# RWKV6 attention and a mixture of adapters: tiles of 64 tokens of two sequences, r and k held transposed

## The chip, the cores and the metric

The kernel runs on one core of a Trainium2 chip. The metric is the device time of one execution in microseconds (us), the median of the runs. The core has five engines with instruction streams of their own: PE (TensorE, the matrix array of 128 rows by 128 columns), DVE (VectorE), ACT (ScalarE), POOL (GpSimd) and SP (SyncE, which here only issues transfers). They meet through semaphores. PSUM is the accumulator memory that PE writes; SBUF is the working memory.

## The reference

Linear attention with a decay per channel (4 batches, 8 heads, 768 tokens, 48 channels per head), then a mixture of adapters over the 3072 tokens with all heads side by side (384 columns). All inputs and the output are fp32.

```python
for t in range(S):                                          # attention, state: (B, H, D, D)
    cur = np.einsum('bhd,bhe->bhde', u[None] * kt, vt)
    y[:, :, t] = np.einsum('bhd,bhde->bhe', rt, state + cur)
    state = wt[:, :, :, None] * state + np.einsum('bhd,bhe->bhde', kt, vt)
...
logits = x @ w_gate                                         # x = y as (3072, 384); 8 experts
topk = np.argpartition(-logits, K, axis=1)[:, :K]           # K = 2
sel = np.take_along_axis(logits, topk, axis=1)
w = np.exp(sel - sel.max(-1, keepdims=True))
w /= w.sum(-1, keepdims=True) + 1e-09
for e in range(E):
    z = x[mask] @ A[e]                                      # 384 -> 16
    delta[mask] += w[mask, k, None] * (z @ B[e])            # 16 -> 384
return x + delta
```

## The kernel before

The recurrence is done in chunks. With P the prefix sum of log w along the tokens of a chunk, r is multiplied by exp(P - centre) and k by exp(centre - P). The attention inside a chunk is then a masked product (r k^T) v, and what earlier chunks give is r times the state. The state S is accumulated as k^T v in PSUM over all chunks of a sequence; the prefix sums run on through the sequence by a second matmul on the chunk before, so nothing has to be rescaled. The term with u is computed apart, as a number per token and head, r.(u k), times v.

**Tiles.** A tile is 128 tokens of one sequence with all 8 heads: 24 tiles, 6 for each of the 4 sequences, one sequence after the other. Tokens lie on the partitions, (head, channel) along the free side. These are the steps of a tile, each a function of the same name:

- `load_w` (two tiles, L168), `load_rk` (r and k, 128x768 fp32, one DMA, L178) on SP; `load_v` (groups of `VGROUPS`, cast to fp16 on the way, L183) on POOL's queue.
- `ln` and `ln1` (ACT, two tiles at once, L245, L254), `cs` (the prefix sums for r and for k, four matmuls of 384 columns with triangular matrices, L257), `exps` (ACT, 128x768, fp32 out, L269), `mult` (DVE, r and k times the exponentials, fp32 in, bf16 out, L274). The output has 64 columns for each head of 48; the padding is set to zero once (memset, L230, four buffers).
- `tr` and `trev`: r and k are transposed, two heads at a time, by 8 PE transposes of 128x128 (L307), and copied out by ACT (128x1024, L316). Afterwards heads of even number lie on partitions 0 to 47, those of odd number on 64 to 111.
- `amm` (8 matmuls of 48 rows, 128x128 out, L321), `aev` (DVE, the mask, 128x1024, L331).
- `kv` (8 matmuls of 64 columns each onto the state, L337, L344), `sev` (ACT, the state to bf16, L347).
- `ymm`: 4 matmuls of r and the state (96 columns, L358) and 8 of the masked products and v (48 columns, L364), all into one PSUM tile y_ps.
- `rkp` (POOL, r times k, L282), 3 transposes of it, `dgmm` (3 matmuls with u, L287), `dgev` (ACT, two tiles, L294), `dv` (POOL, v times that number, L301).
- `xev` (DVE, dv + y_ps to xs, fp16, L368): the tile's attention output.
- `xk` (L374): 3 transposes of xs, and with them the 3 of the rkp of the tile `LEAD` = 3 ahead; `xkev` (L382): their copy, by ACT and DVE in turn.
- `lgmm` (the gate's logits, L393). For a batch of tiles (`BATCHES`, four as a rule): `gate` (ACT, L398), `gmax` (DVE, L405), `gsel` (POOL, four small operations, L417), `zmm` (x times all A, L426), `zw` (DVE, times the gate, L435), `zT` and `zTev` (its transposes, copied by DVE, L444, L452).
- `dmm` (identity times xs, plus zT times all B, into d_ps, L459), `oev` (ACT, to res, L465), `store` (SP, one DMA of 192 KB per tile, L470).

**Order.** The order in which each engine gets its instructions is written by hand. `plan` (L127) gives step f of tile t the due time t + `OFFSET[f]` + `EXTRA[f, t]`, sorts all of them and emits them in that order; the scheduler keeps it on PE, ACT, DVE, POOL and SP. An engine that waits holds up all that stands behind it on its own queue. PSUM tiles are named buffers: one each for cs_ps, s_ps (the state, the logits and the numbers of the u term), trp and a_ps, and a pair with the tag "y" that serves y_ps, xk_ps, z_ps, zT_ps and d_ps in turn.

Of the kernel before, what the change touches and what calls it, by code (L numbers as in the profile page):

```python
# [8 lines left out]
F32 = mybir.dt.float32  # L9
# [9 lines left out]
NCHUNK = 6  # L19
NTILE = 24  # L20
AHEAD = 12
BATCHES = (4, 4, 4, 4, 4, 3, 1)

LEAD = 3
VGROUPS = {0: 1, 1: 3, 4: 4, 8: 4, 12: 4, 16: 4, 20: 4}
VBUFS = {4: 5}
STAGES = ("load_w", "load_rk", "load_v", "ln", "ln1", "cs", "exps", "mult", "rkp", "dv", "tr", "trev", "amm",
          "aev", "kv", "sev", "ymm", "xev", "xk", "xkev", "lgmm", "dgmm", "dgev", "adapters", "casts", "gate", "gmax",
          "gsel", "zmm", "zw", "zT", "zTev", "dmm", "oev", "store")
BATCHED = ("gate", "gmax", "gsel", "zmm", "zw", "zT", "zTev")  # L30

OFFSET = dict(
    load_w=-14.300,
    load_rk=-12.200,
    load_v=7.854,
    ln=9.443,
    ln1=9.187,
    cs=10.060,
    exps=10.665,
    mult=11.280,  # L40
    rkp=9.834,
    dv=13.417,
    tr=11.584,
    trev=12.172,
    amm=12.458,
    aev=12.748,
    kv=12.759,
    sev=13.487,
    ymm=13.577,
    xev=13.957,  # L50
    xk=14.425,
    xkev=14.657,
    lgmm=14.807,
    dgmm=11.851,
    dgev=12.302,
    adapters=-10.500,
    casts=11.924,
    gate=14.935,
    gmax=15.088,
    gsel=15.729,  # L60
    zmm=15.649,
    zw=16.167,
    zT=16.307,
    zTev=16.550,
    dmm=19.950,
    oev=20.325,
    store=159.956,
)
EXTRA = {
    ("load_v", 1): 1.652, ("load_v", 4): 2.471, ("load_v", 20): 0.905,  # L70
    ("ln", 0): -7.731,
    ("cs", 3): 0.370, ("cs", 19): 0.400, ("cs", 21): 0.100,
    ("exps", 4): -0.041,
    ("rkp", 20): 1.472, ("rkp", 21): -0.694,
    ("tr", 3): 0.115,
    ("trev", 1): -0.304, ("trev", 22): -0.410,
    ("amm", 1): -0.099,
    ("aev", 4): -0.018, ("aev", 22): 0.545, ("aev", 23): 0.306,
    ("kv", 22): 0.906, ("kv", 23): -0.729,
    ("sev", 22): 0.179,  # L80
    ("ymm", 20): 0.145, ("ymm", 22): -0.144,
    ("xk", -1): -0.293, ("xk", 0): 0.103,
    ("xkev", -2): 0.186, ("xkev", 2): 0.189,
    ("lgmm", 0): 1.315, ("lgmm", 2): 0.440, ("lgmm", 20): 0.808, ("lgmm", 23): 0.194,
    ("dgmm", 0): 0.907, ("dgmm", 3): 0.277,
    ("dgev", 23): 0.038,
    ("gate", 23): 0.088,
    ("gmax", 19): 0.423,
    ("zmm", 19): 0.638, ("zmm", 22): 0.554,
    ("zw", 19): 0.159, ("zw", 22): 0.214, ("zw", 23): 0.051,  # L90
    ("zT", 19): 0.119, ("zT", 22): 0.576,
    ("zTev", 19): 0.208, ("zTev", 22): 0.664,
    ("dmm", 19): -0.366,
}
TAG = {("d", NTILE - 2): "y", ("d", NTILE - 1): "a_ps", ("z", NTILE - 1): "trp"}
XK_ENG = ("ACT", "DVE")


def batches():
    at, lag, t0 = {}, {}, 0  # L100
    for n in BATCHES:
        at[t0 + n - 1] = (t0, n)
        for t in range(t0, t0 + n):
            lag[t] = t0 + n - 1 - t
        t0 += n
    return at, lag


def runs(f, t, gate_at):
    if f in BATCHED:  # L110
        return t in gate_at
    if f in ("kv", "sev"):
        return t % NCHUNK != NCHUNK - 1 or f == "kv" and t == NTILE - 1
    if f in ("adapters", "casts", "ln1"):
        return t == 0
    if f in ("ln", "load_w"):
        return t % 2 == 0 and not (f == "load_w" and t == 0)
    if f == "load_rk":
        return t > 0
    if f == "load_v":  # L120
        return t > 0 and t in VGROUPS
# [17 lines left out]
def kernel(  # L139
# [28 lines left out]
    def load_w(t):  # L168
        w_in = io.tile([L, 2, HD], F32, name="w_in", bufs=(AHEAD + 4) // 2)
        for i in range(2):  # L170
            st[t + i]["w"] = w_in
# [354 lines left out]
```

## Time and profile before

| | |
|---|---|
| median of 3 runs | 106.34 us (105.53 to 106.39) |
| the profiled execution, its own time: span from first to last instruction | 103.7 us |
| matmuls on PE | 1350, each with a weight load |
| DMA issues | 24 loads of r and k and 24 stores of 192 KB among them |

The profile is one execution, recorded by the hardware; its span runs from the first to the last recorded instruction. The median of the runs stands 2.6 us above that span.

A row of the timeline gives an instruction's (or a group's) start and length in us, its engine, its line in the kernel, the operation, the tile written and the tiles read, their shape (partitions x elements) and type, and a count. For PE, "48*128" ahead of a shape is the part of the array in use, rows times columns. In a table of groups the shape is followed by the count, then by busy time and the mean of one in ns, then by the idle time ahead of them and what ended it. Matmuls overlap, so a group's length is less than its count times the mean of one.

### The profile page before, as it was taken

To read this page: it belongs to the slowest core of one execution; us is meant where nothing else is said; L and a number is where in the kernel's file an instruction comes from. 1 tells how busy PE (TensorE), PEld (TensorE's weight loads), DVE (VectorE), ACT (ScalarE), POOL (GpSimd) and SP (SyncE) were. 2 spreads that over 40 slices of the span, in tenths; PEclk is the share of its full clock that TensorE was granted. 3 is DMA by queue.
4 is the path that set the end of the run, shared out by engine and by line. 5 is a ranking of instruction groups with operands and counts; after the bars stand their busy time and mean duration, and the time that the engine had idled before them with its cause. 6 is when DMAs were issued, how large, how long until landed. Compare 5 with 4: busy or idle time off the path is not lost.

```text
span 103.7 us, 3388 instructions
## 1 busy us (share of the span) xinstructions
PE 85.7 (83%) x1350; PEld 61.8 (60%) x1350; DVE 84.5 (81%) x147; ACT 81.2 (78%) x140; POOL 66.0 (64%) x99
## 2 busy tenths in 40 slices
PE   3455985999198999999968999999999999768640
PEld 0114564777085877777846787777877786645310
DVE  5516599899749999999999999989999999965600
ACT  4525997899559889999996999999999998444360
POOL 5716486959349799787971978939879072613300
PEclk9999999999999999999999999999999999999996
DMA  2999999999999999999659220179201222203353
GB/s 88 203 363 403 380 315 368 404 345 304 340 304 335 410 395 386 341 310 353 216 52 185 82 76 28 54 91 212 77 8 73 81 81 76 79 6 127 145 188 146
DMA packets 13679, 21.86 MB, mean 211 GB/s; under 512 B 1120, under 2 KB 10592, under 8 KB 13664
## 3 DMA queue, kind: packets, MB, share of 16 engines
q1 hardware_dynamic: 10480, 19.30, 51.1%
q0 software_dynamic: 3184, 2.36, 16.1%
q8 instruction: 10, 0.16, 0.7%
q14 instruction: 5, 0.04, 0.1%
HBM read 19.29 MB, written 4.72 MB: 231 GB/s over the span
## 4 chain that ended last, share of the span: by engine, by line
PE 32%; DMA 32%; DVE 15%; ACT 8%; issue 6%; SPq 1%; POOL 1%; ACTq 1%; DVEq 0%; POOLq 0%
DMA v_4_370<-in_v_dram 10%; DMA rk_in<-in_rk_dram 9%; DMA out_dram<-res 8%; DMA w_sb<-in_weights_dram 5%; PE trp L312 5%; DVE rk_1_121 L276 4%; DVE xs L370 3%; PE cs_ps L267 3%; PE cs_ps L265 3%; PE xk_ps L379 3%; ACT res L467 2%; PE a_ps L327 2%; PE d_ps L461 2%; PE s_ps L344 2%; PE z_ps L431 2%
## 5 line engine op out<-in xcount | busy, mean ns | idle before, releaser
L333 DVE TENSOR_TENSOR at<-a_ps,at_mask 128x1024 f16<-128x1024 f32 x24 | 29.2, 1216 | 2.1 <-PE a_ps L327 2.0
L284 POOL TENSOR_TENSOR rkp<-rk_in 128x384 f16<-128x384 f32 x24 | 23.9, 997 | 6.2 <-DMA rk_in<-in_rk_dram 6.0
L318 ACT COPY rkT<-trp 128x1024 bf16<-128x1024 bf16 x24 | 24.5, 1021 | 2.4 <-PE trp L312 2.2
L370 DVE TENSOR_TENSOR xs<-dv,y_ps 128x384 f16<-128x384 f32 x24 | 13.0, 543 | 1.4 <-PE s_ps L395 1.3
L467 ACT COPY res<-d_ps 128x384 f32<-128x384 f32 x24 | 11.6, 488 | 3.2 <-PE d_ps L462 2.7
L349 ACT CAST S_sb<-s_ps 128x384 bf16<-128x384 f32 x20 | 9.8, 488 | 2.9 <-PE s_ps L344 2.1
L250 ACT ACTIVATE logw<-w_in 128x768 f16<-128x768 f32 x11 | 9.4, 856 | 3.1 <-DMA w_in<-in_w_dram 3.1
L386 ACT COPY xkT<-xk_ps 128x768 f16<-128x768 f16 (+1 forms) x13 | 9.9, 762 | 0.4 <-PE xk_ps L379 0.2
L327 PE MATMUL a_ps<-rkT 48*128 48x128 bf16 x192 | 9.7, 222 | 0.3 <-ACT rkT L318 0.3
L267 PE MATMUL cs_ps<-logw,strict 128*128 128x384 f16 x24 | 8.3, 348 | 1.4 <-POOL at_mask masks.py:66 1.4
L379 PE MATMUL xk_ps<-ident_86,rkp 128*128 128x128 f16 x72 | 8.3, 226 | 1.2 <-POOL rkp L284 1.2
L388 DVE COPY xkT<-xk_ps 128x768 f16<-128x768 f16 (+1 forms) x14 | 6.9, 492 | 2.7 <-PE xk_ps L379 2.5
L379 PE MATMUL xk_ps<-ident_86,xs 128*128 128x128 f16 x72 | 8.0, 219 | 0.8 <-DVE xs L370 0.5
L267 PE MATMUL cs_ps<-logw,n_incl 128*128 128x384 f16 x24 | 8.4, 351 | 0.0
L461 PE MATMUL d_ps<-xs,ident_86 128*128 128x384 f16 x24 | 7.7, 323 | 0.4 <-ACT res L467 0.3
L265 PE MATMUL cs_ps<-logw,co_strict 128*128 128x384 f16 x20 | 6.8, 341 | 1.5 <-ACT e_210 L271 0.9
L462 PE MATMUL d_ps<-Ball,zT 128*128 128x384 f16 x24 | 7.8, 323 | 0.0
L379 PEld LDWEIGHTS <-xs 128*128 128x128 f16 x72 | 5.2, 97 | 3.9 <-DVE xs L370 1.9
L327 PEld LDWEIGHTS <-rkT 48*128 48x128 bf16 x192 | 5.5, 95 | 3.1 <-ACT rkT L318 0.5
L364 PEld LDWEIGHTS <-at 128*128 128x128 f16 x192 | 7.0, 96 | 0.4
L358 PE MATMUL y_ps<-S_sb,rkT 128*128 128x96 bf16 x80 | 6.8, 208 | 0.4 <-ACT res L467 0.4
L265 PE MATMUL cs_ps<-logw,n_co_incl 128*128 128x384 f16 x20 | 6.9, 346 | 0.0
(165 smaller groups left out, 220.6 us busy)
## 6 DMA issues: line engine op xcount, KB each, us to landing
rk_in<-in_rk_dram SPq DMA_DIRECT2D x24, 384.0 KB, 9.6
out_dram<-res SPq DMA_DIRECT2D x24, 192.0 KB, 1.9
w_in<-in_w_dram SPq DMA_DIRECT2D x11, 384.0 KB, 9.1
w_in<-in_w_dram SPq DMA_DIRECT2D x2, 192.0 KB, 2.4
v_4_370<-in_v_dram POOLq DMA_DIRECT2D x1, 384.0 KB, 10.4
v_4_510<-in_v_dram POOLq DMA_DIRECT2D x1, 384.0 KB, 10.8
v_4_839<-in_v_dram POOLq DMA_DIRECT2D x1, 384.0 KB, 11.3
v_4_1190<-in_v_dram POOLq DMA_DIRECT2D x1, 384.0 KB, 5.4
```

Source lines behind the costliest of these rows:

```text
L265: nc.tensor.matmul(o, lhsT=wa, rhs=st[t - 1]["logw"], start=False, stop=False, skip_group_check=True)
L267: nc.tensor.matmul(o, lhsT=wb, rhs=lw, start=False, stop=True, skip_group_check=True)
L284: nc.gpsimd.tensor_mul(p_, st[t]["rk"][:, 0], st[t]["rk"][:, 1])
L318: nc.scalar.copy(out=rkT, in_=st[t]["trp"])
L327: nc.tensor.matmul(a_ps[:, g, p, :], lhsT=rkT[base:base + D, 1, p, :], rhs=rkT[base:base + D, 0, p, :], start=True, stop=True)
L333: nc.vector.tensor_mul(at, st[t]["a_ps"].rearrange("s g p f -> s (g p) f"), at_mask.to_broadcast([128, H, 128]))
L349: nc.scalar.copy(out=sb, in_=S_acc)
L370: nc.vector.tensor_add(xs, st[t]["dv"].rearrange("p a b -> p (a b)"), st[t]["y_ps"].rearrange("p a b -> p (a b)"))
L379: nc.tensor.transpose(xk_ps[:, 3 * q + j, :], src[:, j * 128:(j + 1) * 128], ident16)
L386: nc.scalar.copy(out=sb[:, lo:hi], in_=st[t]["xk_ps"][:, lo:hi])
L461: nc.tensor.matmul(d_ps, lhsT=ident16, rhs=st[t]["xs"], start=True, stop=False)
L467: nc.scalar.copy(out=res, in_=st[t]["d_ps"])
```

## The change

A tile is now 64 tokens of two sequences at once. There are again 24 tiles, 12 for each pair of sequences (`NCHUNK` = 12). Nothing of what is computed changes.

- **Layout and loads.** The host lays r and k out with channels on the partitions (48 for even heads at 0, 48 for odd heads at 64) and, along the free side, sequence, head pair, r or k, and token: 1024 elements. `load_rk` fetches them in 8 groups (`RKGROUPS`), two DMAs each, on POOL's queue, cast to fp16 into four standing buffers. Tile 0 comes as fp32 by SP. Rows 48 to 63, which no load writes, are set to zero by memsets (`pads`, and some of the start). v and w are laid out so that a tile has 64 tokens of the one sequence above 64 of the other.
- **Prefix sums.** `cs` makes them transposed: for each head pair and sequence one matmul on the tile before (or on a constant) and one on this tile, 64 rows, 128 columns. `exps` reads 112x1024 and writes bf16; `mult` multiplies 112x1024 of 16-bit data; `rkp` is made on DVE out of the same data (112x512). `tr` and `trev` are gone.
- **Attention.** `amm`, `dgmm`, `kv`, `inter` and `intra` (which were `ymm`) become 16 matmuls each, for 2 sequences by 8 heads, on 64x64 quarters of the array. `kv` needs k with tokens on the partitions: `ktr` transposes it (16 of 64x64), `ktev` (DVE) copies it out. The mask product is 128x512.
- **The u term.** `dv` is written as fp16 and `bonus` adds it to y_ps on PE, by four matmuls with the identity. `xev` is then a plain copy, by ACT and DVE in turn.
- **Rest.** `xk` has 3 transposes, its copy is always DVE's. `gsel` is on DVE. `xk_ps`, `k_ps`, `z_ps`, `zT_ps` and `d_ps` share a ring of two PSUM buffers. The prefix sums of a tile lie in two banks, y_ps in two. Each store is two DMAs, of 64 rows. `res` has 8 buffers.
- **Order.** A written list (`ORDER`) takes the place of the due times.

```diff
-NCHUNK = 6
+NCHUNK = 12
+C = 64
-VGROUPS = {0: 1, 1: 3, 4: 4, 8: 4, 12: 4, 16: 4, 20: 4}
+VGROUPS = {0: 2, 2: 2, 4: 4, 8: 4, 12: 4, 16: 4, 20: 4}
+RKGROUPS = {1: (0, 1), 2: (0, 2), 4: (1, 2), 6: (1, 2), 8: (2, 4), 12: (3, 4), 16: (1, 4), 20: (2, 4)}
+RKBUF = {0: 3, 1: 4, 2: 4, 3: 4}
-OFFSET = dict(
...
+ORDER = """
+adapters.0 load_w.1 load_w.3 pads.1 pads.2 pads.3 ln.0 load_v.0 load_rk.1 casts.0 cs.0 ln.1 exps.0 mult.0 load_rk.2
+load_w.5 load_v.2 rkp.0 load_rk.4 cs.1 ln.3 exps.1 load_v.4 load_rk.6 rkp.1 cs.2 amm.0 mult.1 rkp.2 dgmm.0 ktr.0
+dgmm.1 exps.2 dgev.1 cs.3 dv.0 aev.0 intra.0 ktr.1 load_w.7 dv.1 ktev.0 exps.3 bonus.0 xev.0 dgmm.2 kv.0 mult.2
...
+dgmm.8 ktev.8 intra.7 xkev.6 bonus.7 dgmm.9 amm.8 sev.7 dmm.0 xev.7 mult.9 xk.7 lgmm.6 load_v.12 cs.10 oev.0 ktr.9
+dgev.9 rkp.10 inter.8 kv.8 aev.8 dv.8 xkev.7 exps.10 store.0 rkp.11 load_w.13 dv.9 amm.9 intra.8 bonus.8 dgmm.10
...
+zT.22 store.11 gmax.23 gsel.23 zTev.22 oev.17 zmm.23 dmm.18 zw.23 dmm.19 oev.18 zT.23 oev.19 store.12 dmm.20 zTev.23
+store.13 dmm.21 store.14 oev.20 dmm.22 store.15 oev.21 oev.22 dmm.23 store.16 oev.23 store.17 store.18 store.19
+store.20 store.21 store.22 store.23
+"""
...
+    nc.vector.memset(logws[0][:, :, :, D:], 0.0)
+    nc.vector.memset(rkbuf[0][32:64, 0:1], 0.0)
...
+    nc.vector.memset(rkbuf[0][32:64, 1:3], 0.0)
...
     def load_rk(t):
-        rk_in = io.tile([L, 2, HD], F32, name="rk_in")
-        nc.sync.dma_start(out=rk_in, in_=rk[t])
+        b, n = RKGROUPS[t]
+        o = t - 1 if b == 0 else t % 4
+        for g in range(2):
+            nc.gpsimd.dma_start(out=rkbuf[b][g * 64:g * 64 + D, o:o + n], in_=rk[g, :, t:t + n])
...
+    def pads(t):
+        nc.vector.memset(rkbuf[t][32:64], 0.0)
...
     def cs(t):
...
+        for p in range(P):
+            for b in range(2):
+                s = slice(b * 64, b * 64 + 64)
+                o = cs_ps[:, b, p].rearrange("a r t -> a (r t)")
+                if c == 0:
+                    nc.tensor.matmul(o, lhsT=ones[s, :], rhs=centre[s].rearrange("a r t -> a (r t)"),
+                                     start=(p == 0), stop=False, skip_group_check=True)
+                else:
+                    nc.tensor.matmul(o, lhsT=pre[s, p], rhs=carry[s].rearrange("a r t -> a (r t)"),
+                                     start=False, stop=False, skip_group_check=True)
+        for p in range(P):
+            for b in range(2):
...
+                nc.tensor.matmul(o, lhsT=lw[s, p], rhs=cur[s].rearrange("a r t -> a (r t)"),
+                                 start=False, stop=True, skip_group_check=True)
...
+    def mult(t):
+        rk2 = wk.tile([128, 2, P, 2, C], BF16, name="rk2", bufs=4)
+        nc.vector.tensor_mul(rk2[0:112].rearrange("a b p r t -> a (b p r t)"), st[t]["rk"][0:112],
+                             st[t]["e2"][0:112].rearrange("a b p r t -> a (b p r t)"))
...
+    def ktr(t):
+        k_ps = pp.tile([128, 2, P, D], BF16, name="k_ps", tag="ring", bufs=2)
+        for b in range(2):
+            for p in range(P):
+                for g in range(2):
+                    nc.tensor.transpose(k_ps[rows(g, 64), b, p, :], rk2[rows(g), b, p, 1, :],
+                                        identb[rows(g), 0:D])
...
+    def inter(t):
+        for p in range(P):
+            for b in range(2):
+                for g in range(2):
+                    nc.tensor.matmul(y_g[g][rows(b, 64), p, :], lhsT=d["rk2"][rows(g), b, p, 0, :],
+                                     rhs=st[t - 1]["S"][rows(g), p, b, :], start=(p == 0), stop=False,
+                                     skip_group_check=True)
...
+    def bonus(t):
+        for b in range(2):
+            for g in range(2):
+                nc.tensor.matmul(y_ps[rows(b, 64), g, 0:P * D], lhsT=ident[rows(g, 64), rows(g, 64)],
+                                 rhs=d["dv"][rows(g, 64), b].rearrange("s p d -> s (p d)"), start=False, stop=True,
+                                 skip_group_check=True)
...
     def store(t):
-        nc.sync.dma_start(out=out[t * 128:(t + 1) * 128, :], in_=st[t]["res"])
+        q, c = divmod(t, NC)
+        for b in range(2):
+            nc.sync.dma_start(out=out_v[q, c, b], in_=st[t]["res"][rows(b, 64)])
```

In `amm`, `ktr`, `dgmm` and `kv` the quarters used alternate between the upper left and the lower right of the array; in `inter` and `intra` they go round all four. (`intra` has the loops of `inter`, with the masked products and v.)

More of the change, by code (lines that the diff above doesn't have):

```diff
@@ L32 @@
-OFFSET = dict(
[L33 to L94, printed above, removed]
@@ L331, in aev @@
[L331 to L345 removed]
+        dv_ = wk.tile([L, 2 * P, D], FP16, name="dv", bufs=3)
@@ L376, in xk @@
[L376 to L379 removed]
+        xk_ps = pp.tile([128, 3, 128], FP16, name="xk_ps", tag="ring", bufs=2)
+        for j in range(3):
+            nc.tensor.transpose(xk_ps[:, j, :], st[t]["xs"][:, j * 128:(j + 1) * 128], ident)
         st[t]["xk_ps"] = xk_ps
```

465 lines of the change are left out of this document (243 added, 222 removed).

## The prediction

> **What bounds the kernel now.** I read the page's busy times first, then the pace of one operation through the span, then the timelines of PE, DVE and ACT inside the even stretch. Columns of a timeline are start, length (us), engine, line, operation.
>
> ```profile
> span 103.7 us, 3388 instructions
> ...
> PE 85.7 (83%) x1350; PEld 61.8 (60%) x1350; DVE 84.5 (81%) x147; ACT 81.2 (78%) x140; POOL 66.0 (64%) x99
> ```
> ```profile
> 16.72 0.54 DVE L370 TENSOR_TENSOR xs<-dv,y_ps 128x384 f16<-128x384 f32 x1
> ```
> ```profile
> 30.40 1.21 DVE L333 TENSOR_TENSOR at<-a_ps,at_mask 128x1024 f16<-128x1024 f32 x1
> 31.53 0.54 DVE L370 TENSOR_TENSOR xs<-dv,y_ps 128x384 f16<-128x384 f32 x1
> 31.99 0.36 DVE L412 MAX8 top<-ge 128x8 f32<-128x8 f32 x4
> ...
> 32.68 0.93 DVE L276 TENSOR_TENSOR rk_3_125<-rk_in,e_645 128x768 bf16<-128x768 f32 x1
> ...
> 35.12 0.68 DVE L438 TENSOR_TENSOR zw<-z_ps,g 128x512 f16<-128x512 f32 x1
> ...
> 36.59 0.41 DVE L455 COPY zT<-zT_ps 128x512 f16<-128x512 f16 x1
> 36.93 0.54 DVE L388 COPY xkT<-xk_ps 128x768 f16<-128x768 f16 x1
> ```
> ```profile
> 93.83 0.55 DVE L370 TENSOR_TENSOR xs<-dv,y_ps 128x384 f16<-128x384 f32 x1 [1.33 <-PE s_ps L395]
> ```
> The first xs (tile 0) starts at 16.72, that of tile 4 at 31.53, the last at 93.83. So there is a start of 16.7, a slow ramp, an even stretch of 62.3 us for 19 tiles, 3.28 each, and a tail of 103.7 - 93.8 = 9.9. DVE's starts follow each other about 0.08 sooner than its lengths say (at 31.53 - 30.40 = 1.13, xs 0.46, and so product 0.85, zw 0.60, zT 0.33, xkT 0.46). A batch of four tiles has 0.69 for its maxima (31.99 to 32.68), a zw and a zT: 0.41 per tile. DVE's sum per tile is 1.13 + 0.85 + 0.46 + 0.23 (every second xkT) + 0.41 = 3.08.
>
> ```profile
> 64.39 0.40 PE L327 MATMUL a_ps<-rkT 48*128 48x128 bf16 x8
> 64.72 0.34 PE L358 MATMUL y_ps<-S_sb,rkT 128*128 128x96 bf16 x4
> 64.90 0.36 PE L364 MATMUL y_ps<-v_4_839,at 128*128 128x48 f16 x8
> 65.11 0.61 PE L312 MATMUL trp<-ident,rk_0_119 128*128 128x128 bf16 x8
> 65.64 0.31 PE L344 MATMUL s_ps<-v_4_839,rk_3_125 128*64 128x48 f16 x8
> 65.88 0.23 PE L395 MATMUL s_ps<-w_72,xkT 128*128 128x8 f16 x3
> ...
> 66.05 0.32 PE L461 MATMUL d_ps<-xs,ident_86 128*128 128x384 f16 x1
> 66.21 0.32 PE L462 MATMUL d_ps<-Ball,zT 128*128 128x384 f16 x1
> ```
> ```profile
> L327 PE MATMUL a_ps<-rkT 48*128 48x128 bf16 x192 | 9.7, 222 | 0.3 <-ACT rkT L318 0.3
> L344 PE MATMUL s_ps<-v_1_73,rk_0_119 128*64 128x48 f16 x8 | 0.3, 194 | 0.0
> L364 PE MATMUL y_ps<-v_4_839,at 128*128 128x48 f16 x32 | 1.5, 184 | 0.0
> ```
> A group's length less one matmul's mean, over one less than its count, is the spacing. The full array (128*128) takes 25 ns for 48 columns ((0.36 - 0.184) / 7), 45 for 96, 56 for 128 and 160 for 384 (66.21 - 66.05). The two groups that use part of the array are faster than their size: a_ps, whose heads alternate between rows 0 and 64, takes 26 ns for 128 columns, and s_ps of L344, alternating between column halves, 17 for 48. So two matmuls run side by side there. Entering or leaving such a group costs about 0.09 more: the last a_ps starts at 64.57, would take 0.056, and the next group starts only at 64.72; trp should be through at 65.56, L344 starts at 65.64.
>
> With these, PE's work per tile is cs 0.65, xk 0.34, a_ps 0.21, y_ps 0.35, trp 0.45, L344 0.11, logits and bonus 0.16, d_ps 0.32, z 0.22, resets 0.03, changes of array 0.33, in all 3.17: 97% of the pace. PE sets it, with DVE close behind.
>
> **The change, part by part.** *PE.* 1350 matmuls become 3010, by the loops. At the measured spacings: cs is 384 with 64 rows and 128 columns, in pairs of row halves like a_ps, at 26 ns: 10.0. The six groups of 64x64 (ktr, amm, dgmm, intra 384 each, kv and inter 352) are 2240 matmuls of 1 to 64 columns; amm, ktr, dgmm, kv pair opposite corners of the array, so I take L344's 17 ns: 38.1. The bonus, 96 of 192 columns, two at a time, 41 each: 3.9. The rest stays on the full array: xk 4.0, z 5.3, logits 1.8 (at 25), d_ps 7.7. The new order changes the array's division 90 times, at 0.09: 8.1. Sum 78.9, or 3.29 per tile, against 3.17 now. The transposes of r, k and rkp are gone (10.8 + 4.0), and what replaces them costs as much. Bounds: inter and intra walk all four corners, so four might run together, 8.5 ns instead of 17 (736 matmuls, -6.3); at the 25 ns of the full array's row the six groups cost +17.9. I take 17, since rows with a divided array are the nearest.
>
> *DVE.* The mask product halves to 128x512: 0.61 (zw). The product with the exponentials is now 1024 elements of two bytes, from SBUF, 112 rows. Between at (1024) and zw (512) an element costs 1.02 ns, fixed 0.09; so at most 1.13.
>
> ```profile
> L455 DVE COPY zT<-zT_ps 128x512 f16<-128x512 f16 x5 | 2.1, 422 | 0.5 <-PE zT_ps L448 0.4
> L388 DVE COPY xkT<-xk_ps 128x384 f16<-128x384 f16 x4 | 1.4, 340 | 0.0
> L455 DVE COPY zT<-zT_ps 128x128 f16<-128x128 f16 x1 | 0.2, 226 | 0.3 <-PE zT_ps L448 0.3
> ```
> Copies of f16 cost (422 - 226) / 384 = 0.51 ns per element; at that the product takes 0.61. I take 0.61, because operand width is what these copies share with it; likewise rkp (512, now on DVE), 0.35 rather than 0.61. Then ktev and xkev 0.26 each, half the xev 0.23, the gate's share with gsel moved in 0.54: 2.86 per tile, or 3.64 at the upper prices. Add 0.2 for stalls:
> ```profile
> 52.13 2.59 DVE L276 TENSOR_TENSOR rk_1_121<-rk_in,e_1178 128x768 bf16<-128x768 f32 x1
> ```
> ```profile
> 52.10 0.84 POOL L303 TENSOR_TENSOR dv<-v_4_510,dg 128x384 f32<-128x384 f16 x1
> 52.89 1.00 POOL L284 TENSOR_TENSOR rkp<-rk_in 128x384 f16<-128x384 f32 x1
> ```
> This product, 1.6 longer than the others, began beside two products on POOL and ended 0.9 after them, as if it had waited for both. POOL now has one per tile.
>
> The Trainium skill, "VectorE: DVE Perf Modes", section "The perf-mode tier table", says that a two-input operation on two-byte SBUF data runs at two elements per cycle and on fp32 at one. By that the product is an estimated 0.6, by the at row 1.13; no run here shows such an operation yet, the copies' slope agrees.
>
> *ACT* loses the copy of trp and its xkT copies.
> ```profile
> 70.28 0.89 ACT L250 ACTIVATE logw<-w_in 128x768 f16<-128x768 f32 x1
> 71.02 0.52 ACT L349 CAST S_sb<-s_ps 128x384 bf16<-128x384 f32 x1
> 71.38 0.87 ACT L271 ACTIVATE e_1686<-cs_ps 128x768 f32<-128x768 f32 x1
> ```
> By their starts half a logw is 0.37 and S 0.36; res, of the same size, 0.36, half an xev 0.18; exps of 1024 instead of 768 at most 0.87 x 4/3, less the overlap of 0.16 that S shows, 1.0; small ones 0.1: 2.37 per tile, against 3.28. ACT is cover, not bound.
>
> *Queues and loads.* POOL gives up rkp and gsel, and issues 16 more loads.
> ```profile
> L303 POOL TENSOR_TENSOR dv<-v_4_1190,dg 128x384 f32<-128x384 f16 x4 | 4.1, 1017 | 2.3 <-ACT dg L297 2.3
> L186 POOL DMA_DIRECT2D v_4_1190<-in_v_dram x1 | 0.8, 822 | 0.0
> q1 hardware_dynamic: 10480, 19.30, 51.1%
> q0 software_dynamic: 3184, 2.36, 16.1%
> ```
> 23 x 0.82 + 24 x 1.02 = 43 us: cover. A load of rk waits for its buffer, with dv queued behind it, but the buffers it reuses (tile 16 takes that of tiles 4 to 7) were left two tiles earlier. Casting traffic triples: 3 x 16.7 = 50 us of the 16 engines, the other queue falls from 53 to about 27; 77 in all, spread over the span, so loads are not the bound after the start.
>
> *Start.* On DVE some 8,400 elements of memset and eight small copies now come ahead of the first product.
> ```profile
> 2.00 0.48 DVE L230 MEMSET rk_0_119<- 128x512 uint32 x1
> 2.54 0.48 DVE L230 MEMSET rk_1_121<- 128x512 uint32 x1
> ```
> One of 512 takes 0.54 from start to start, 0.88 ns per element behind the fixed 0.09 found above. That is 7.4 for the elements, 1.0 for eleven fixed parts and 1.2 for the copies (0.15 each, 64 at 1.02 ns and 0.09), from about 0.9, so 10.5. Behind it stand product 1.13 (fp32), rkp 0.61, rkp 0.35, product 0.61, rkp 0.35, mask 0.61: 14.2, first xev at 14.8, the second 2.4 later at 17.2 (ktev, product, rkp, ktev, mask, xkev lie between them on DVE, 2.35). Its loads, 3.8 MB at q1's 364 GB/s (19.30 MB in 53 us), are in by 12.
>
> *Tail.* Each store becomes two.
> ```profile
> L471 SPq DMA_DIRECT2D out_dram<-res x24: 332/332/413, 41.5 to 100.7; - x24
> ```
> ```profile
> 99.13 1.93 SPq L471 DMA_DIRECT2D out_dram<-res  x4
> ```
> ```profile
> out_dram<-res SPq DMA_DIRECT2D x24, 192.0 KB, 1.9
> ```
> Eight tiles' outputs come after the last xev: 16 issues, at between 0.33 (one's length) and 0.53 (the last four now, (1.93 - 0.33) / 3), I take 0.42, nearer the length: 6.7, from 1.3 after that xev (xk 0.34, d_ps 0.48, res 0.49), and 1.9 to land: 9.9. The last tile's own chain to its result, some twelve steps, is an estimated 5.3 and so shorter. So the tail stays 9.9; SP is its bound instead of PE and ACT.
>
> *Sum.* Of PE's 78.9, 5.4 lies ahead of the second xev (four cs, and 14 other groups) and 3.8 behind the last one (eight d_ps, two z groups, the last logits). 69.7 at the 97% of today is 72. 17.2 + 72 + 9.9 = 99.1, against the span of 103.7. The runs' median is 106.34, 2.6 above that span; with it, 101.7. I say 101, because the one price in it that lies at its upper bound, four corners, can only lower it. All of the gain is start and ramp; PE's even stretch is no shorter per tile.
>
> **Rivals.** *Four corners at once* (against the forecast's two): PE falls to 63.5 in the stretch, DVE with 22 x 3.06 = 67 becomes the bound: 17.2 + 67 + 9.9 + 2.6 = 97. For it, L344 and a_ps show both halvings separately; against, no row has both.
>
> *Instruction supply, slower.* 6020 PE instructions instead of 2700; 5,390 in the stretch. From 64.39 to 65.88 the trace has 72 (36 matmuls with their weight loads) in 1.49 us, 21 ns each; the L344 burst alone has 16 at 8.5. The forecast needs 13.4 without pause. From 14.4 on the change is slower than 107.4; at the 21 of those 72 the stretch would be 113 and the time 143, halfway, at 17, 92 and 121. For: nothing longer than a burst was that fast. Against: the array explains the 21 by itself.
>
> The Trainium skill, "Runtime: NRT & Kernel Launch", section "Instruction fetch mechanics", speaks against the change: about 20 cycles per instruction to dispatch, an estimated 16.7 ns at its 1.2 GHz. The L344 burst at 8.5 ns does not agree, but that may be what had queued up; by the page the time would be about 120.
>
> *Products at one element per cycle.* DVE 3.84 per tile, 84.5 in the stretch: 114. Against it the copies' slope.
>
> *No change*: waits between the small groups cost PE 8% more, 107.
>
> **How the numbers follow.** Forecast 0.45 (its own range 98 to 106), four corners 0.20, supply 0.18, slow products 0.09, no change 0.08. A measurement of this kernel tells about 1% from no change. Faster than 105.3: the four corners and nearly all of the forecast, 0.62; within 1%, 0.08; slower 0.30. The range 94 to 115 reaches from the four corners to the slow products and leaves out most of the supply case and a DVE without stalls.
>
> **What would show it.** 64x64 groups of 16 in about 0.27 + a length (four corners: near 0.14); the product at 0.6 to 0.7 long; ACT busy under 65; xs of tile 0 at 15, the last near 89; a store issue every 0.42 in the tail. I am wrong if PE shows many gaps ended by nothing (supply), if DVE has no idle time, or if PE waits for rk loads past 20 us.

## The result, and the profile after

The changed kernel takes 138.16 us (median of 4 runs, 137.2 to 141.81) against 106.37 before (105.53 to 106.52): 1.298 times as long, with a 95% interval of 1.287 to 1.310. (Ratios, here and below, leave out the runs of either kernel that took over 1.5% longer than its fastest.) The forecast was 101. The profiled execution has a span of 135.5 us, 36.4 more than the forecast's 99.1, and all three terms of the sum are short:

| | before | forecast | measured |
|---|---|---|---|
| start, to the second xs | 20.4 | 17.2 | 26.2 |
| stretch, to the last xs | 73.4 | 72 | 93.4 |
| tail | 9.9 | 9.9 | 15.9 |

The column "before" is read from the second xs of that kernel and from its last one, at 93.83:

```profile
20.42 0.54 DVE L370 TENSOR_TENSOR xs<-dv,y_ps 128x384 f16<-128x384 f32 x1
```

In the timelines of the changed kernel the first two of these lines are ACT's and DVE's copies of y_ps for tiles 0 and 1, the third is the last one:

```profile
21.57 0.48 ACT L216 CAST xs<-y_ps 128x384 f16<-128x384 f32 x1
...
26.16 0.56 DVE L218 CAST xs<-y_ps 128x384 f16<-128x384 f32 x1 [1.23 <-PE y_ps L412]
...
119.59 0.56 DVE L218 CAST xs<-y_ps 128x384 f16<-128x384 f32 x1 [0.24 <-PE y_ps L389]
```

The page of the changed kernel, with busy tenths, the clock granted to PE and the transfers in 40 slices of 3.4 us:

```profile
span 135.5 us, 6695 instructions
...
PE 92.7 (68%) x3010; PEld 74.3 (55%) x3010; DVE 87.3 (64%) x236; ACT 64.1 (47%) x117; POOL 34.4 (25%) x55
...
PE   1210399838997397976599939959979877974400
...
PEclk9999999999999959999655896586899999999965
DMA  4999996993029170399921753961722222234453
GB/s 126 247 264 282 233 274 144 191 186 66 5 39 186 19 121 5 75 293 212 278 64 29 197 156 46 220 151 18 168 66 63 63 63 58 54 72 116 119 145 88
...
q0 software_dynamic: 2032, 6.88, 28.4%
...
q8 instruction: 23, 0.38, 1.2%
```

No engine is full: PE is busy for 68% of the span, DVE for 64%. PE's row has holes in the middle of the stretch, and PE's timeline shows what ends them:

```profile
26.95 0.50 PE L402 MATMUL xk_ps<-ident,xs 128*128 128x128 f16 x3
...
27.73 0.56 PE L319 MATMUL a_ps<-rk 48*64 48x64 bf16 x13
30.86 0.26 PE L319 MATMUL a_ps<-rk 48*64 48x64 bf16 x2 [2.58 <-issue]
...
42.87 0.84 PE L447 MATMUL z_ps<-w,xT 128*128 128x128 f16 x12
...
43.63 0.33 PE L402 MATMUL xk_ps<-ident,xs 128*128 128x128 f16 x3
...
44.44 0.31 PE L371 MATMUL y_ps<-S_sb,rk 48*64 48x48 bf16 x16
44.59 0.42 PE L319 MATMUL a_ps<-rk 48*64 48x64 bf16 x16
44.84 0.29 PE L357 MATMUL s_ps<-v,kt 64*48 64x48 f16 x9
47.42 0.26 PE L357 MATMUL s_ps<-v,kt 64*48 64x48 f16 x7 [2.30 <-issue]
```

At 28.3 PE stops in the middle of a group: 13 of the 16 matmuls of a_ps are done, the other three come 2.6 us later, and nothing that the profile knows had been missing ("issue"). At 45.1 the same happens after 9 of 16. So, it seems, the operands were there and the instructions were not; the runs below test that. Counted by windows that begin and end at such stops (matmuls and weight loads of each, then DVE, ACT and POOL, the clock, the transfers):

```profile
core 0: us, PE busy (x) PEld busy (x) DVE busy (x) ACT busy (x) POOL busy (x), PEclk, DMA share, GB/s
42.05:47.41 5.36, 3.08 (x128) 2.75 (x128) 3.62 (x11) 2.31 (x4) 2.33 (x3) 1.00 0.51 90
47.41:52.24 4.83, 4.04 (x128) 3.32 (x128) 2.92 (x7) 2.73 (x4) 0.00 (x0) 0.65 0.53 85
...
59.42:65.89 6.47, 3.82 (x128) 3.26 (x128) 4.03 (x11) 2.80 (x5) 2.61 (x3) 0.94 1.04 261
103.40:106.85 3.45, 3.09 (x128) 2.49 (x128) 3.08 (x8) 2.69 (x5) 0.00 (x0) 1.00 0.32 76
106.85:110.58 3.73, 2.84 (x128) 2.39 (x128) 3.17 (x6) 2.33 (x5) 1.80 (x2) 1.00 0.25 60
110.58:114.31 3.73, 2.86 (x128) 2.34 (x128) 2.92 (x15) 2.07 (x4) 0.00 (x0) 1.00 0.24 55
```

Each stretch between two stops has 128 + 128 = 256 instructions. That is the unit in which they are fetched: q8 moved 0.38 MB in 23 packets, 16.4 KB each, one for 262 of PE's 6020 instructions. Put beside each other, the packet records and PE's starts give the following (us). A "page" is such a stretch of 256; a "stop" is counted here from the last start of one page to the first of the next, so that it holds the 0.2 of a matmul beside the idle time.

```
page begins  stop before it  fetch of next begins  lasts  next page begins
 24.12        0.88            27.71  (+3.59)        1.68    30.86
 42.05        0.89            44.47  (+2.42)        1.59    47.42
 59.43        1.09            63.22  (+3.79)        1.25    65.90
 85.17        0.00            88.76  (+3.60)        1.41    91.67
 99.68        1.20           100.81  (+1.13)        1.25   103.41
106.86        0.53           108.11  (+1.25)        1.24   110.59
110.59        1.07           111.74  (+1.15)        1.26   114.32
```

Where PE stands at a page end, it goes on 1.2 to 1.5 us after the fetch has ended. Where few transfers run, the fetch begins 1.1 to 1.3 us after the page end, so that in this kernel a page costs at least 3.45 to 3.73 us however fast the array is. Beside the loads it begins up to 3.8 us after it. The stops at the 23 page ends add up to 20.3 us, 19.4 of them in the stretch; of idle time alone they hold 17.2.

The second finding is the clock. Three transposes take 0.50 at 26.95 and 0.33 at 43.63; the last two starts are 107 ns apart in the first group and 55 in the second. PE ran at half clock until 37.8 us (the page's clock row, which has no record before that, shows full there), and again for 24 us in four pieces from 48 to 96. Each of these pieces began right after 3.4 us in which PE was busy for less than half, that is with one of the long stops.

### The profile page after: what moved, and what is told of

The parts are those of the page before. It is cut to its first block, busy times and chain, and to the rows that moved or that the text cites. A ratio compares the mean times of both kernels' runs of the same rounds, so it can differ in the third digit from the quotient of the medians.

```text
span 135.5 us, 6695 instructions
## 1 busy us (share of the span) xinstructions
PE 92.7 (68%) x3010; PEld 74.3 (55%) x3010; DVE 87.3 (64%) x236; ACT 64.1 (47%) x117; POOL 34.4 (25%) x55
## 4 chain that ended last, share of the span: by engine, by line
PE 62%; issue 14%; DMA 9%; DVE 5%; ACT 2%; SPq 2%; ACTq 0%; DVEq 0%
DMA w_in<-in_w_dram 9%; PE cs_ps L270 7%; PE k_ps L305 7%; PE a_ps L319 6%; PE s_ps L331 5%; PE cs_ps L276 5%; PE xk_ps L402 5%; PE s_ps L357 5%; PE y_ps L371 4%; PE d_ps L477 4%; PE y_ps L381 4%; PE y_ps L389 3%; PE d_ps L478 3%; PE z_ps L447 2%; PE y_ps L412 2%
## 5 line engine op out<-in xcount | busy, mean ns | idle before, releaser
L343 POOL TENSOR_TENSOR dv<-v,dg 128x384 f16<-128x384 f16 x24 | 21.0, 891 | 79.2 <-ACT dg L337 75.4
L281 ACT ACTIVATE e<-cs_ps 112x1024 bf16<-112x1024 f32 x24 | 24.6, 1024 | 8.9 <-PE cs_ps L276 8.8
L324 DVE TENSOR_TENSOR at<-a_ps,cur 128x512 f16<-128x512 f32 x24 | 16.4, 685 | 5.0 <-PE a_ps L319 4.9
L286 DVE TENSOR_TENSOR rk<-rk,e 112x1024 bf16<-112x1024 f16 x23 | 16.7, 725 | 0.3 <-ACT e L281 0.3
L305 PE MATMUL k_ps<-identb,rk 48*64 48x48 bf16 x384 | 12.6, 203 | 3.9 <-issue 3.5
L319 PE MATMUL a_ps<-rk 48*64 48x64 bf16 x384 | 12.3, 210 | 3.6 <-issue 3.6
L276 PE MATMUL cs_ps<-cur,logw 64*128 64x128 f16 x192 | 12.8, 267 | 2.4 <-DVE cur L188 2.4
L270 PEld LDWEIGHTS <-logw 64*128 64x128 f16 x176 | 6.6, 112 | 12.6 <-issue 11.8
L305 PEld LDWEIGHTS <-rk 48*64 48x64 bf16 x384 | 10.4, 127 | 5.3 <-issue 4.8
L319 PEld LDWEIGHTS <-rk 48*64 48x64 bf16 x384 | 10.2, 125 | 4.8 <-issue 4.3
L293 DVE TENSOR_TENSOR rkp<-rk 112x512 f16<-112x512 f16 x23 | 11.8, 527 | 0.0
L276 PEld LDWEIGHTS <-logw 64*128 64x128 f16 x192 | 9.1, 122 | 3.1 <-issue 2.6
```

What stands on the lines that cost most here:

```text
L270: nc.tensor.matmul(o, lhsT=pre[s, p], rhs=carry[s].rearrange("a r t -> a (r t)"), start=False, stop=False, skip_group_check=True)
L276: nc.tensor.matmul(o, lhsT=lw[s, p], rhs=cur[s].rearrange("a r t -> a (r t)"), start=False, stop=True, skip_group_check=True)
L281: nc.scalar.activation(out=e2[0:112], in_=cs_ps[0:112], func=ACT.Exp)
L286: nc.vector.tensor_mul(rk2[0:112].rearrange("a b p r t -> a (b p r t)"), st[t]["rk"][0:112], st[t]["e2"][0:112].rearrange("a b p r t -> a ...
L293: nc.vector.tensor_mul(p_[0:112], src[:, :, 0, :], src[:, :, 1, :])
L305: nc.tensor.transpose(k_ps[rows(g, 64), b, p, :], rk2[rows(g), b, p, 1, :], identb[rows(g), 0:D])
```

## The experiments

"The changed kernel" is the one predicted. Times are medians, with the range of 4 runs (the two kernels with PE instructions only ran once); the kernel before took 107.2, 106.9 and 105.9 us beside the three sets that were timed.

**Same instructions, less for the array to do.**

The edit in amm, whose m is 8 after the first tile; cs, kv, inter, intra and bonus are cut in the same way:

```diff
-                    nc.tensor.matmul(a_ps[rows(g, 64), b * P + p, :], lhsT=rk2[rows(g), b, p, 1, :],
-                                     rhs=rk2[rows(g), b, p, 0, :], start=True, stop=True, skip_group_check=True)
+                    nc.tensor.matmul(a_ps[rows(g, 64), b * P + p, 0:m], lhsT=rk2[rows(g), b, p, 1, :],
+                                     rhs=rk2[rows(g), b, p, 0, 0:m], start=True, stop=True, skip_group_check=True)
```

> The changed kernel with the same PE instructions, but most of them with few columns: prefix sums 16 instead of 128, masked products 8 instead of 64, state, inter and intra 8 instead of 48, bonus 16 instead of 192, from the second chunk on (so most of the attention is left out). Theory A (pages): the number of instructions is the same, so pages still take at least 3.5 us each and the gaps at their ends grow by what the array saves; 138 falls by at most 8. Theory B (array): per tile at least 1.0 us of array work goes at full clock and twice that at half clock, so the time falls by 25 us or more, to under 113.

Measured: 142.02 (141.12 to 143.78), 4 us more than the changed kernel, with most columns gone. Theory B (the array) is out by 29 us. The first stops are there at the same places of the order:

```profile
42.75 1.46 PE L453 MATMUL z_ps<-w,xT 128*128 128x128 f16 x12
...
45.52 0.34 PE L360 MATMUL s_ps<-v,kt 64*48 64x8 f16 x9
47.98 0.29 PE L360 MATMUL s_ps<-v,kt 64*48 64x8 f16 x7 [2.12 <-issue]
```

That it became slower was not expected: z_ps, which was left alone, takes 1.46 instead of 0.84, and the transposes stay 107 ns apart to the end. PE did not leave half clock before 128 us. So theory A was not met in full either: its stops were to grow, and they add up to 13.6 instead of 20.3. From 100 us on there are hardly any, with pages of 3.6 to 5.5 us and PE busy nearly throughout, and there the run cannot tell the array at half clock from the pages. It shows that fewer columns did not help; that pages set the pace rests on the runs that follow.

**Same instructions, no loads beside them.**

```diff
     def load_rk(t):
         b, n = RKGROUPS[t]
+        if t > 7:
+            for i in range(n):
+                st[t + i]["rk"] = st[4 + i]["rk"]
+            return
```

load_v has the same lines, and load_w from tile 7 on.

> The changed kernel without the loads of r, k, v (from tile 8 on) and w (from tile 7 on): those tiles work on the data of tiles 4 to 7 (and on the w of tiles 5 and 6), so that after about 30 us only the stores move data. The instructions of PE are the same. Theory A with C (PE waits for its pages, and a fetch queues behind loads): fetches start 1.0 to 1.6 us after the page end, the 19 pages after tile 3 take 3.5 to 3.8 us each instead of 4.5, gaps stay at about 1 us, no gap is over 1.5 us and with them the half-clock stretches after tile 3 are gone; 17 to 20 us less, 118 to 121, which is still above the 106 of the kernel before: that rest is the number of instructions. If the loads only happened to run at those times, the time stays near 138.

Measured: 121.95 (120.73 to 123.98), 1.144 times before (1.133 to 1.156): 16 us less than the changed kernel, a little less than forecast. Three pages of its stretch, in windows:

```profile
81.32:85.04 3.72, 2.94 (x128) 2.45 (x128) 3.37 (x16) 3.07 (x6) 0.00 (x0) 1.00 0.33 79
85.04:88.77 3.73, 3.51 (x128) 2.85 (x128) 3.44 (x9) 2.17 (x5) 1.66 (x2) 1.00 0.16 36
88.77:92.50 3.73, 3.08 (x128) 2.49 (x128) 3.36 (x9) 2.69 (x5) 0.00 (x0) 1.00 0.32 77
```

The 12 pages from 59.6 to 103.4 take 3.65 each. No stop is longer than 1.4 us, all stops add up to 10.9 instead of 20.3, and the clock, once full at 43.7, stays full to the end of the work. The second xs and the last one were

```profile
25.70 0.56 DVE L218 CAST xs<-y_ps 128x384 f16<-128x384 f32 x1 [1.23 <-PE y_ps L425]
...
105.13 0.56 DVE L218 CAST xs<-y_ps 128x384 f16<-128x384 f32 x1 [0.24 <-PE y_ps L402]
```

so that the stretch is 79.4, and the tail 15.9 as in the changed kernel. The profiled execution of the changed kernel is 31.7 us longer than that of the kernel before: 20.0 in the stretch, 5.7 in the start, 6.0 in the tail. Of the 20.0, 14.0 go with the loads, together with the half clock that followed the long stops, which this run does not take apart. The other 6.0 fit the pages alone: the 5,390 instructions of the stretch are 21 pages, 77 us at 3.65. Start and tail hardly move.

**The fetch beside loads, by itself.** Two kernels with PE instructions only, 768 matmuls of 8 columns on the full array and 1536 on quarters, without and with the changed kernel's loads of r and k, asked for one after another ahead of the work.

```diff
+    for i in range(14):
+        big = io.tile([128, 4, 1024], FP16, name="big")
+        for g in range(2):
+            nc.gpsimd.dma_start(out=big[g * 64:g * 64 + 48], in_=rk[g, :, 4 * (i % 6):4 * (i % 6) + 4])
```

> Not the reference's computation (its output is left as zeros): PE alone, with nothing to wait for. First 768 matmuls of 8 columns on the full array, then 1536 of 8 columns in the upper left and lower right quarter in turn; no loads. Theory A (pages): the first part goes at the full array's 25 ns per matmul, 6.4 us for 256 instructions with the weight loads, without gaps; the second would go at 8 to 17 ns per matmul by the array, but comes at 3.45 to 3.75 us per 256 instructions, with a gap of about 1 us every 256, the same as in the quiet part of the changed kernel. Theory B (PE takes instructions one by one at some rate, or the gaps are waits that the profile doesn't name): no gaps, an even spacing in the second part.

> The same PE stream, with the changed kernel's loads of r and k for four tiles (two casting DMAs of 48 rows by 8 KB) asked for without end beside it, into two buffers that nothing reads. Theory C (a page fetch queues behind the bytes asked for before it): the fetch of each page starts 2.5 to 4.5 us after the page end before it instead of 1.1, pages in the second part take 5 to 7 us, 12 pages some 70 us instead of 43; the first part, too, goes slower than 6.4 us per page at times. If fetches are served beside the loads, 3.5 to 4 us per page.

Without loads (81.0 us) there was little to see: a matmul started every 26.7 ns in both parts, 3.41 us for 128 of them. (The expectation's 6.4 us for the first part counted instructions as matmuls.) That is only just shorter than a page, and the stops at the page ends of the second part are 0.07 to 0.60. This kernel does not tell the theories apart. With loads (112.6 us) the same stream reads, in PE's timeline:

```profile
10.63 3.55 PE L148 MATMUL f_ps<-x,wt 128*128 128x8 f16 x128 [3.41 <-issue]
15.18 3.56 PE L148 MATMUL f_ps<-x,wt 128*128 128x8 f16 x128 [1.00 <-issue]
22.20 3.56 PE L148 MATMUL f_ps<-x,wt 128*128 128x8 f16 x128 [3.46 <-issue]
29.49 3.55 PE L148 MATMUL f_ps<-x,wt 128*128 128x8 f16 x128 [3.73 <-issue]
```

Every 128 matmuls PE stands for up to 3.7 us, with no semaphore in sight. Pages take 4.6 to 7.3 us and fetches begin 1.4 to 4.2 us after the page end; as soon as the loads end, at 69.7 us, pages are back at 3.45 to 4.0.

**Smaller and spread loads.** First the loads of one tile each at the old places (packets of 2 KB instead of up to 8), then also spread, one tile's loads per tile (r, k and v, from tile 8 on). The edit for the first:

```diff
-RKGROUPS = {1: (0, 1), 2: (0, 2), 4: (1, 2), 6: (1, 2), 8: (2, 4), 12: (3, 4), 16: (1, 4), 20: (2, 4)}
+RKGROUPS = {t: ((0 if t < 4 else 1 + (t // 4 - 1) % 3), 1) for t in range(1, 24)}
```

> The changed kernel, with the loads of r and k asked for one tile at a time (46 DMAs of 2 KB per row in place of groups of up to 8 KB per row), at the same places of the order. Theory A (pages): PE's instructions come in pages of 256 and PE stands at each page end until the next has been fetched; a fetch starts 1.1 us after the page end when no load runs, and 2.4 to 3.8 us after it beside the 8 KB packets of the r and k loads. With small packets the late fetches should start 1.1 to 2 us after the page end, the gaps ended by nothing fall from 19 us to about 12, the half-clock stretches that follow the long gaps get fewer, and the time falls from 138 to about 125 to 132. Theory B (PE is bound by the array's own work at the granted clock; the gaps only use up time in which PE would have waited for data): within 2 us of 138. Theory C (fetches queue behind whole loads, whatever the packet size): within 2 us too, with the fetches as late as before.

> The changed kernel with the loads of r, k and v from tile 8 on asked for one tile at a time and spread over the order, one tile's loads per tile, instead of four tiles' at once. With small packets at the same places the page fetches beside the loads still started 2.4 to 4.0 us after the page end, near the end of the loads: they seem to queue behind what was asked for before them. Theory C (a fetch queues behind the bytes already asked for): now at most one tile's 0.3 MB stand ahead of it, late starts are 1.1 to 2.2 us, pages in the middle take 3.6 to 4.6 us instead of up to 6.7, and the time falls by 6 to 10 us, to 130. If the lateness came from elsewhere (PE's own waits for data in the page before), the time stays within 2 us of 138.

Measured: 134.73 (132.13 to 136.13) and 135.04 (134.81 to 136.3; 1.281 times before, 1.270 to 1.293). Packet size does not bring the fetch forward: with small packets it still begins up to 4.0 us after the page end, 2.4 or more at seven of them, which speaks for theory C, though the 3 us gained are more than C allowed and less than A forecast. Spread, late starts are 1.7 to 3.6, more pages have one, and the stops add up to 16.8 instead of 20.3. For both runs the gain that the pages were to give was forecast too large. A likely reason, not tested, is that the same bytes stand ahead of some fetch either way.

**Fewer instructions.** Once without the term with u (rkp, dgmm, dgev, dv and bonus), with filler for the array in its place; once with the prefix sums of both sequences in one matmul, which computes the whole.

```diff
     def dgmm(t):
...
+        for i in range(6):
+            nc.tensor.matmul(s_ps[:, 2 * P * D:], lhsT=ident, rhs=carry.rearrange("a r t -> a (r t)"), start=False,
+                             stop=True, skip_group_check=True)
```

```diff
-                nc.tensor.matmul(o, lhsT=lw[s, p], rhs=cur[s].rearrange("a r t -> a (r t)"),
+            nc.tensor.matmul(o, lhsT=lw[:, p], rhs=cur2.rearrange("a b r t -> a (b r t)"), start=False, stop=True,
+                             skip_group_check=True)
```

> The changed kernel without the term with u (rkp, dgmm, dgev, dv and bonus are left out), and in dgmm's place six matmuls of 128 columns on the full array, whose result is used by nothing. Per tile that is 28 PE instructions fewer (40 out, 12 in; 670 in all, 2.6 pages), while the array's work is about the same (out: 16 matmuls of one column in 0.25 us, 4 of 192 columns in 0.15; in: 6 at 56 ns, 0.34). Theory A (PE waits for pages of 256 instructions): 2.6 pages at the 4.3 us that a page took in the middle of the changed kernel, 11 us less, 127. Theory B (the array's work): within 3 us of 138. If the chain through POOL (dv) had held the tiles up, the time would fall by more than the pages give.

> The changed kernel with the prefix sums of both sequences in one matmul: 128 rows and 256 columns with a block-diagonal mask instead of two of 64 rows and 128 columns that run side by side; 8 instead of 16 matmuls per tile, 184 instead of 368 in all, so 368 PE instructions fewer (1.4 pages). The array's work grows: 8 x 107 ns = 0.86 us per tile instead of the 0.60 measured at full clock, 6 us in all. The rest is as it was, and the result is complete. Theory A (pages): 1.4 pages of 4.3 us, 6 us less, 132. Theory B (array): 5 to 6 us more, 144.

Measured: 130.64 (125.86 to 132.75), 7.5 less for 2.6 pages, between the 11 of theory A and the 3 of B; its runs scatter, but all four are below the lowest of the changed kernel, 137.2. The gain cannot be put down to the instructions alone, since rkp, dgev and dv, which went with the term, had kept DVE, ACT and POOL busy too. And 136.37 (130.12 to 139.96): the sign of A, but its runs scatter by more than the difference, so this one decides nothing.

**The clock by itself.** 16 matmuls of 512 columns in PE's idle time at the start.

```diff
+        for i in range(16):
+            nc.tensor.matmul(w_ps, lhsT=tri, rhs=logws[0][:, 0].rearrange("s h d -> s (h d)"), start=True, stop=True,
+                             skip_group_check=True)
```

> The changed kernel with 16 matmuls of 512 columns more in the idle time of PE between the first prefix sums (7.2 us) and the second (14.5 us); their result is used by nothing. In the changed kernel PE ran at half clock until 37.8 us (transposes 107 ns apart instead of 56). Theory B (clock): with the array busy ahead of the first tiles the clock is full from about 15 us on, the work between 15 and 38 us takes 6 to 9 us less, 138 falls to 130. Theory A (pages): the first page ends come about 1 us sooner, but behind them PE waits for pages just as long; 138 falls by 0 to 3, and the clock halves again after the first long gap.

Measured: 137.82 (136.79 to 138.69), no gain. The clock was full from 10.0 to 16.9 us, then half again until 47.6. The full clock did not last: in the 3.4 us before 16.9 PE, waiting for ACT's exponentials, was busy for a fifth of the time. So the run shows that this filler does not help, and not what a full clock from 17 to 38 us would be worth.

**Start and tail.** First the steps of the start in another order, then that, the spread loads and a second queue for the stores together.

```diff
-adapters.0 load_w.1 load_w.3 pads.1 pads.2 pads.3 ln.0 load_v.0 load_rk.1 casts.0 cs.0 ln.1 exps.0 mult.0 load_rk.2
+load_w.1 ln.0 load_v.0 load_rk.1 cs.0 exps.0 mult.0 adapters.0 load_rk.2 load_w.3 rkp.0 ln.1 cs.1 amm.0 exps.1 rkp.1
...
-            nc.sync.dma_start(out=out_v[q, c, b], in_=st[t]["res"][rows(b, 64)])
+            (nc.sync, nc.scalar)[b].dma_start(out=out_v[q, c, b], in_=st[t]["res"][rows(b, 64)])
```

> The changed kernel with another order of the first 45 steps alone: the first tile's exponentials go ahead of the casts and of the second log on ACT, the weights' load goes behind the first load of w, the memsets of the later buffers and the loads of r, k and v that come after tile 3 go behind the first tiles' work. In the changed kernel ACT stood on the load of w until 12.7 us with the first exponentials queued behind it, and the first copy of y (tile 0) came at 21.6, the second at 26.1. Theory A (the start is a matter of what is queued ahead of the first exponentials, and the pages come after it): first copy of y at 11 to 13, second at 16 to 18, and the whole time 7 to 9 us less, 130. Theory B (pages and loads bound the start too): under 3 us less.

> The changed kernel with both of the edits before (order of the start, spread loads), and with the second half of each store issued by ACT instead of SP. In the changed kernel the last 14 issues on SP, 0.56 us each, end the kernel. Theory A: the gains add up, 8 for the start, 6 to 8 for the loads and 3 to 4 for the tail: 118 to 121. If the pages alone set the pace from the first tile on, a sooner start only moves the waits: about 128.

Measured: 136.44 (136.26 to 138.56; 1.292 times before, 1.285 to 1.299) and 134.24 (132.35 to 136.56; 1.258, 1.244 to 1.272). With the new order the first two copies of y came at

```profile
17.63 0.47 ACT L214 CAST xs<-y_ps 128x384 f16<-128x384 f32 x1
...
23.28 0.56 DVE L216 CAST xs<-y_ps 128x384 f16<-128x384 f32 x1
```

4.0 and 2.9 us sooner, but the last one at 118.7 only 0.9 sooner: with two late page fetches beside the loads (pages of 7.3 us at 25.1 and 56.8) the stretch was 2.0 longer. Together with the other two edits the last copy came at 114.8 and the tail was 16.7, no shorter than 15.9: ACT's last seven issues then stood 0.66 us apart.

**One DMA per store**, whose target is two pieces of 64 rows.

```diff
-        for b in range(2):
-            nc.sync.dma_start(out=out_v[q, c, b], in_=st[t]["res"][rows(b, 64)])
+        nc.sync.dma_start(out=out_v[q, c], in_=st[t]["res"])
```

> The changed kernel with each store as one DMA of 128 rows again, instead of two of 64. In the changed kernel a tile's two issues take 1.29 us of SP, and the last eight tiles' stores end the kernel; 15.9 us lie behind the last copy of y. Theory A: with 24 issues of 0.33 to 0.5 the tail is bound by ACT and PE again, about 4 us shorter, 134. Theory B (the writes themselves, not their issue, set the tail): within 1 us of 138.

Measured: 174.17 (171.48 to 174.66), neither of the two; see the last section.

## Why the prediction was wrong, step by step

- **The products and copies on DVE and ACT: right.** Groups of the changed kernel:

```profile
L286 DVE TENSOR_TENSOR rk<-rk,e 112x1024 bf16<-112x1024 f16 x23 | 16.7, 725 | 0.3 <-ACT e L281 0.3
...
L281 ACT ACTIVATE e<-cs_ps 112x1024 bf16<-112x1024 f32 x24 | 24.6, 1024 | 8.9 <-PE cs_ps L276 8.8
```

  The product took 0.60 from start to start (forecast 0.61, not 1.13), ACT is busy for 64.1 us (forecast: under 65). The Trainium skill, "VectorE: DVE Perf Modes", section "The perf-mode tier table", has two elements per cycle for such operands; this trace agrees, with 1024 elements in 0.60 us.
- **PE's array work: the forecast was too high.** By the rows at 44.44 and 44.59 and the means of their groups (203 and 210 ns), (0.31 - 0.20) / 15 = 7 ns per matmul of inter, which goes round four corners, and 14 for a_ps, which uses two. That is the rival's four corners. From 110.59 on the 256 instructions of a page ran in 2.6 us, for about one tile; the forecast had 3.29 per tile. So the array had room to spare.
- **The instruction supply: the step that failed.** The text set it aside with "the array explains the 21 by itself", and the sum took PE's time from array prices alone. The forecast needed 13.4 ns per instruction without pause; the threshold was put at 14.4. A page of 3.45 to 3.73 us is 13.5 to 14.6 ns, just there, when no load runs; the stretch had 93.4 us for 5,390, 17.3 ns. The rival's own figure for 17 was a stretch of 92. So the mechanism had a price and a place in the text, and got 0.18. Two readings went wrong. A burst of 16 instructions, such as that of L344, says what the array takes from instructions that are there, nothing on the supply of thousands. And "nothing longer than a burst was that fast" was the only evidence on supply in the trace, and it was counted as weak. The profile of the kernel before did show the fetches: its q8 row has one packet of 16 KB per 256 or so instructions, there about every 8 us:

```profile
q8 instruction: 10, 0.16, 0.7%
```

  That a page costs 3.5 us could not be read from it, nor that a fetch comes late beside loads. What the runs showed in place of the 72 us is a stretch of 93.4, which is 79.4 without the late loads: of the 21 us that were missing, 7 go with the pages and 14 with the late fetches and the half clock behind them.
- **What spoke against the change.** The Trainium skill, "Runtime: NRT & Kernel Launch", section "Instruction fetch mechanics", says that instructions come in blocks of 256 and that the next is fetched while the current one runs: the trace agrees. It calls the cost of a block's end mostly hidden, since dispatch takes about 20 cycles per instruction; here neither holds. After a stop PE ran 256 instructions at 10 ns, and the ends cost 20.3 us. The estimate of 120 from its 16.7 ns came near the stretch that was measured, for another reason.
- **Loads: "not the bound after the start" was right as a sum of bytes** (q0 and q1 take 56% of the engines' span) **and wrong in effect**: two DMAs of r and k for four tiles, such as

```profile
38.86 1.08 POOL L232 DMA_DIRECT2D rk<-in_rk_dram  x2
...
rk<-in_rk_dram POOLq DMA_DIRECT2D x8, 384.0 KB, 7.1
```

  take 7 us to land (the median of the eight). Those two moved data from 40.1 to 45.6 by their packet records, and the fetch due after the page end at 42.05 came at 44.47, when they were nearly through. No line of the forecast had a transfer that stands in another's way.
- **Start: 9.0 too short.** The loads came at 126 to 282 GB/s in the first five slices, not 364, and ACT's order put the second log, which waits for w, ahead of the first exponentials:

```profile
12.74 0.84 ACT L253 ACTIVATE logw<-w_in 128x768 f16<-128x768 f32 x1 [2.69 <-DMA w_in<-in_w_dram]
13.49 1.01 ACT L281 ACTIVATE e<-cs_ps 112x1024 bf16<-112x1024 f32 x1
...
14.55 0.61 PE L270 MATMUL cs_ps<-carry,logw 64*128 64x128 f16 x8 [7.35 <-ACT e L281]
```

  The forecast had followed DVE's queue alone. With another order the second xs came 2.9 sooner. The rest of the 9 was not taken apart; PE at half clock and a page fetch that began 2.8 us after the page end (at 21.72) fall into it.
- **Tail: 6.0 too short.** SP issued the last stores

```profile
124.98 7.87 SPq L489 DMA_DIRECT2D out_dram<-res  x12
```

  0.66 us apart (forecast 0.42): 16 times the difference is 3.8. The other 2 are what is left, a later begin of these issues in the main. Why an issue takes longer here is open; a second queue did not help. The tail was 15.9 us, too, without the late loads and with spread ones, so that the loads do not lengthen it.

In sum the change loses twice by its number of instructions: 6020 of them are 23.5 pages of 3.5 us or more, and each fetch that stands behind a load adds up to 2.7. Without the late loads it is still slower than the kernel before (122 against 106), and if the 15 us by which start and tail missed the forecast were won back on top of that, an estimate, it would be at 107.

## What to carry to other kernels

Count PE's instructions, weight loads included, beside the array's time: 256 of them took about 3.5 us at best here, page after page (single pages that followed a slower one took as little as 2.8 in other runs), so matmuls that the array does in less than 27 ns each, with their weight loads, did not pay. Where a timeline has stops ended by nothing, count the instructions from one to the next; 256 is the sign of a fetch. And large transfers delay these fetches, so a kernel near that rate has to keep its loads out of the way, which smaller packets did not do here.

## What the runs showed of the hardware that was not expected

- In the changed kernel each stop of about 2 us or more that began at full clock was followed by half clock for 3.4 to 10 us, and in the kernel with few columns PE did not get the full clock before 128 us (107 ns between transposes to the last of them, at 125), though it was busy for nearly all of several stretches of 3.4 us.
- One store DMA whose target is two pieces went at 50 to 54 GB/s once the loads were over, where the changed kernel, with two DMAs, has 72 to 145 at the end. About a tenth of the DMA engines' time was busy, and the tail took 50.3 us instead of 15.9:

```profile
DMA  5999999209160497511881811111111111111110
GB/s 165 228 246 255 270 191 182 47 10 170 17 95 4 133 211 164 110 52 54 242 175 45 168 51 54 54 54 54 54 50 50 50 50 50 50 50 50 50 50 35
```
